# A ring place cleared behind every second transfer in a row, and two low parts moved from GpSimd to VectorE

## The chip, the cores and the metric

The kernel runs on one core of a Trainium2 chip, in one launch. The metric is the device time of that launch in microseconds (us), measured without a profiler. Besides, one execution was recorded by the hardware profiler; its clock starts at the first recorded instruction. The engines go by these names: PE is TensorE (PEld its weight loads), DVE is VectorE, ACT is ScalarE, POOL is GpSimd, SP is SyncE, which here only issues transfers.

## The reference

Pooled attention with 8 batches, 8 heads, 576 tokens, head width 64, followed by a routed feed-forward layer with 8 experts. All is float32.

```
k_p, v_p = mean over groups of 8 keys (576 -> 72)
attn     = softmax(q k_p^T / 8);  x = attn v_p        # 4608 tokens of 512 numbers
compute  = x @ w_skip > 0                              # the other tokens keep x
e        = argmax(x @ w_gate), g = its probability     # 8 experts
out      = x + g * (relu(x @ w1[e]) @ w2[e])           # 512 -> 1024 -> 512
```

## The kernel before, in words

**Numbers in two parts.** The expert products multiply float32 as a high and a low part: `whi` is the weight rounded by ACT (`high`, line 600), `wlo` the weight minus `whi` (`low` on POOL, line 603, or `low_v` on DVE, line 608). A chunk of weights (`cc` 0 to 7, 512 KB each; 0 to 3 are of w1, 4 to 7 of w2) comes from DRAM into a place of `stage`; each chunk is split in two halves `i` of 128 x 512.

**First stage: 36 tiles of attention.** The loop at line 866 takes one tile of 128 tokens a turn `t`, with scores, exponentials, transposes and values of different tiles overlapped. Tiles are routed in groups of 9, 5, 4, 6, 5, 4 and 3 (`route`, line 385): DVE finds each token's expert, PE counts ranks, DVE makes the places `r_di`, and POOL then writes one indirect transfer for each tile (line 433), which scatters 128 rows of 32 bytes (token number and gate weight) into `table` in DRAM. After the first group one expert is picked, the *early expert*. Three tiles of its tokens, from the first 18 tiles, are gathered by POOL at turn 30 (line 512) and computed while the routing ends; the writes of later tiles wait until those tokens are known.

**The order on POOL and DVE is planned when the program is built.** `Work` (line 642) holds items with the turn from which they can run, the turn at which they are due, and a cost; each turn it takes items up to a budget. `Spaced` (line 663) does this for POOL, and holds the table writes and the three gathers apart as `writes`. A write is taken if at least 1.2 us (`APART`) of other planned work was taken since the last one, or if no other item can run and the write is due. The writes of a group are due in successive turns. From turn 26 on, `fill` is set to `clear` (line 790): before a write that follows another one closely it puts a memset of one of the ring places 3 to 5 (128 x 516 numbers). These places must be zero before the experts stage, each at least once. After the last attention tile the rest is taken in two calls (lines 934 and 943), and the three writes of the last group in a third (line 982), where `fill` is off.

**Low parts.** `later_low` (line 702) is called when a half's high part is made. The first halves (`i` = 0) of chunks 2 to 6 and both of chunks 0 and 1 go to POOL; the second halves of chunks 2 to 6 go to DVE; chunk 7 is done after the routing on DVE (line 993). The first halves of chunks 5 and 6 have their turn on POOL at turns 33 and 35. When a place of `stage` has been split, SP loads into it a chunk of the second expert (`load_second`, line 590; chunk 7 goes to the place that chunk 5 had, at turn 35).

**From the routing to the experts.** PE has 56 steps of the early expert's two products (line 573) in hand. 36 of them are placed among the last routing work, the last 20 in the experts stage. Once the whole table is written, POOL gathers the rows that say which tokens each unit has (line 1070); PE transposes them (line 1102), DVE copies them to `slot` and `gate`, and after the steps that are left all engines meet at the entry of the experts stage (line 1137). There POOL gathers token rows by `slot` (line 1314), and from then on PE computes unit after unit. The order of PE in the program is fixed: line 1102 stands behind 28 of the 36 steps and ahead of the other 8.

Of the kernel before, what the change touches and what calls it, by code (L numbers as in the profile page):

```python
# [40 lines left out]
NT = NTOK // 128  # L41
# [19 lines left out]
WRITE, APART, REST = 1.27, 1.2, 0.5  # L61
# [27 lines left out]
def chunk_src(w1, w2, e, c):  # L89
    if c < 4:  # L90
        return w1[bass.ds(e, 1)].rearrange("o (p k) n -> k (o p) n", k=4)[c]
    k = (c - 4) * 2
    return w2[bass.ds(e, 1), k * 128:(k + 2) * 128, :].rearrange("o (a p) n -> (o p) a n", p=128)
# [6 lines left out]
def chunk_view(st, c):  # L100
    return st if c < 4 else st.rearrange("p (a n) -> p a n", a=2)
# [62 lines left out]
def attention(tc, nc, q, k, vm, vr, cf, wg, w1, w2, whi, wlo, out, c, pay, offs, table, near, bufs, late, early, mb, fin, cfs):  # L164
    with ExitStack() as ctx:
# [358 lines left out]
        later, now = {}, {}  # L524
# [54 lines left out]
        def expert(i, most=NE - 1):  # L579

            if i not in experts_:
                r = nc.sync.alloc_register(f"expert{i}")
                nc.sync.reg_load(r, near["order"][0:1, i:i + 1])
                experts_[i] = nc.sync.snap(r, min_val=0, max_val=most)
            return experts_[i]

        def room(cc):
            return 5 + cc % 3 if cc < 6 else (0, 5)[cc - 6]

        def load_second(c):  # L590
            nc.sync.dma_start(chunk_view(stage[:, c], c), chunk_src(w1, w2, expert(1), c))

        def load_first(cc):
            assert cc == 6 or len(lows) >= (8 if cc == 7 else 2 * cc - 4), (cc, lows)
            nc.sync.dma_start(chunk_view(stage[:, room(cc)], cc), chunk_src(w1, w2, expert(0), cc))

        def piece(w, cc, i):
            return w[0][:, cc, i * 512:i * 512 + 512] if cc < 4 else w[1][:, (cc - 4) * 2 + i, :]
# [4 lines left out]
        def low(cc, i):  # L603
            lows.append(cc)
            nc.gpsimd.tensor_tensor(piece(wlo, cc, i), stage[:, room(cc), i * 512:i * 512 + 512],
                                    piece(whi, cc, i).bitcast(F32), ALU.subtract)

        def low_v(cc, i):
            lows.append(cc)
            nc.vector.tensor_tensor(piece(wlo, cc, i), stage[:, room(cc), i * 512:i * 512 + 512],  # L610
                                    piece(whi, cc, i).bitcast(F32), ALU.subtract)
# [5 lines left out]
        class Queue:  # L617

            def __init__(self):
                self.gens, self.held = [], False  # L620
# [21 lines left out]
        class Work:  # L642
# [9 lines left out]
            def take(self, t, spent=0.0, most=99):  # L652
                got = [i for i in self.items if i[2] <= t]
                for i in got:
                    if most == 0 or spent + i[3] > self.budget and i[0] > t:
                        break
                    spent += i[3]
                    most -= 1
                    self.items.remove(i)
                    i[4]()  # L660
                return spent

        class Spaced(Work):

            def __init__(self, budget):
                super().__init__(budget)
                self.writes, self.apart, self.hold, self.fill = [], APART, True, None

            def write(self, ready, last, f, early=True):
                self.n += 1  # L670
# [3 lines left out]
            def take(self, t):  # L674
                spent = 0.0
                while True:
                    w = next((i for i in self.writes if i[2] <= t and (i[4] or not self.hold)), None)
                    o = next((i for i in self.items if i[2] <= t), None)
                    late = w is not None and w[0] <= t
                    if w is None and o is None or spent >= self.budget and not late and not (o is not None and o[0] <= t):  # L680
                        break
                    if w is not None and (self.apart >= APART or o is None and late):
                        if self.apart < REST and self.fill:
                            self.fill()
                        self.writes.remove(w)
                        w[3]()
                        spent, self.apart = spent + WRITE, 0.0
                    elif o is not None:
                        self.items.remove(o)
                        o[4]()  # L690
                        spent, self.apart = spent + o[3], self.apart + o[3]
                    else:
                        break

        loads, behind, turns = {}, {}, {}
        lows = []
        act, dve, gps = Work(ACT), Work(DVE), Spaced(GPS)
# [4 lines left out]
        def later_low(cc, i):  # L702
            if cc == 7:
                return
            if cc > 1 and i:
                dve.add(now["t"] + 1, now["t"] + 2, 0.65, lambda: low_v(cc, i))
                return
            gps.add(now["t"] + (2 if cc > 4 else 1), (NT if cc > 5 else wload(cc + 3)) - 1, 1.25, lambda: low(cc, i))

        def adds(b, ready, last):  # L710
            first, small = sums(b)
# [4 lines left out]
        def wload(cc):  # L716
            return PICKED + 9 * cc // 4 if cc < 8 else NT - 2
# [15 lines left out]
        for cc in range(8):  # L733
            (loads if cc else behind).setdefault(wload(cc), []).append(lambda cc=cc: load_first(cc))
            for i in range(2):
                act.add(wload(cc) + (3 if cc < 3 else 4), min(wload(cc) + 6, NT - 2), 0.55, lambda cc=cc, i=i: (high(cc, i), later_low(cc, i)))

        for cc, t in SECOND.items():
            at(t, lambda cc=cc: load_second(cc))
# [21 lines left out]
        o = ps_o.tile([128, 2, 512], F32, name="o")  # L761
# [104 lines left out]
        for t in range(2, NT):  # L866
# [35 lines left out]
            spent = act.take(t, 0.4 if new is not None else 0.0, 2 if t + 1 in FIRST[2:] else 1)  # L902
# [917 lines left out]
```

## Time and profile before

| | |
|---|---|
| median of 3 runs | 483.04 us (481.76 to 483.20) |
| the profiled execution | 483.0 us |
| its span, first to last instruction | 480.9 us |
| mean granted clock of TensorE | 0.993 |
| PE busy | 456.1 us (95%) |
| POOL busy | 251.0 us (52%) |
| DVE busy | 302.1 us (63%) |
| ACT busy | 226.8 us (47%) |

The profiled execution took 483.0 us; 2.1 us of it lie outside the span. Busy shares are means over all stages: POOL has 52% over the span, but in the stage before the experts it hardly rests.

### The profile page before, as it was taken

To read this page: it belongs to the slowest core of one execution; us is meant where nothing else is said; L and a number is where in the kernel's file an instruction comes from. 1 tells how busy PE (TensorE), PEld (TensorE's weight loads), DVE (VectorE), ACT (ScalarE), POOL (GpSimd) and SP (SyncE) were. 2 spreads that over 40 slices of the span, in tenths; PEclk is the share of its full clock that TensorE was granted. 3 is DMA by queue.
4 is the path that set the end of the run, shared out by engine and by line. 5 is a ranking of instruction groups with operands and counts; after the bars stand their busy time and mean duration, and the time that the engine had idled before them with its cause. 6 is when DMAs were issued, how large, how long until landed. Compare 5 with 4: busy or idle time off the path is not lost. (4 is left out here: it accounts for less than half of the span.)

```text
span 480.9 us, 12651 instructions
## 1 busy us (share of the span) xinstructions
PE 456.1 (95%) x3755; PEld 406.7 (85%) x3756; DVE 302.1 (63%) x713; ACT 226.8 (47%) x614; POOL 251.0 (52%) x328
## 2 busy tenths in 40 slices
PE   7899989999989589999999998999999999999995
PEld 4689888888989579888989987989899898989894
DVE  5878898789779113579795657662756654343321
ACT  5678889899951001447462746512435241212110
POOL 4499399999998145335242514352543161515242
PEclk9999999999999799999999999999999999999999
DMA  8999999979720016688677597877687323322021
GB/s 282 399 396 388 400 365 343 389 269 338 255 107 3 9 47 199 219 217 294 246 248 281 169 296 262 316 229 243 197 251 263 99 88 107 128 66 88 22 87 42
DMA packets 52048, 103.98 MB, mean 216 GB/s; under 512 B 10031, under 2 KB 22959, under 8 KB 50336
## 3 DMA queue, kind: packets, MB, share of 16 engines
q1 hardware_dynamic: 40544, 78.18, 47.1%
q0 software_dynamic: 11456, 25.22, 14.9%
q8 instruction: 23, 0.38, 0.3%
q14 instruction: 25, 0.20, 0.1%
HBM read 80.85 MB, written 31.21 MB: 233 GB/s over the span
## 5 line engine op out<-in xcount | busy, mean ns | idle before, releaser
L1319 POOL DMA_INDIRECT out<-ring,slot x33 | 35.4, 1073 | 106.0 <-POOLq L1145 102.9
L331 ACT ACTIVATE e<-sc,mn 128x72 f32<-128x72 f32 x288 | 65.5, 352 | 10.9 <-DVE mn L323 10.2
L1557 ACT ACTIVATE hhi<-psl 128x256 fp32r<-128x256 f32 (+3 forms) x59 | 23.5, 400 | 98.0 <-ACTq L1145 91.8
L1413 PE MATMUL psl<-xhi,w1hi 128*128 128x256 f32 (+3 forms) x220 | 64.0, 291 | 0.0
L1414 PE MATMUL psl<-xlo,w1hi 128*128 128x256 f32 (+3 forms) x220 | 64.0, 291 | 0.0
L1415 PE MATMUL psl<-xhi,w1lo 128*128 128x256 f32 (+3 forms) x220 | 63.9, 291 | 0.0
L1314 POOL DMA_INDIRECT ring<-out,slot x42 | 49.1, 1168 | 24.5 <-issue 24.1
L359 PE MATMUL o<-vbd,pT 128*128 128x148 f32 (+1 forms) x312 | 50.3, 299 | 4.9 <-ACT pT L346 1.8
L1656 DVE SCALAR_TENSOR_TENSOR hlo<-psl,hhi 128x256 fp32r<-128x256 f32 (+2 forms) x55 | 23.2, 423 | 42.9 <-DVEq L1145 39.7
L359 PEld LDWEIGHTS o<-vbd,pT 128*128 128x128 f32 (+1 forms) x312 | 39.2, 179 | 9.0 <-ACT pT L346 4.3
L1413 PEld LDWEIGHTS psl<-xhi,w1hi 128*128 128x128 f32 x220 | 41.3, 188 | 0.8 <-issue 0.4
L1414 PEld LDWEIGHTS psl<-xlo,w1hi 128*128 128x128 f32 x220 | 41.3, 188 | 0.5
L1415 PEld LDWEIGHTS psl<-xhi,w1lo 128*128 128x128 f32 x220 | 41.2, 187 | 0.0
L433 POOL DMA_INDIRECT table<-pay,r_di x36 | 36.3, 1009 | 6.4 <-issue 5.4
L1327 POOL DMA_DIRECT2D sorted<-ring x39 | 22.2, 571 | 32.7 <-DMA ring<-out,slot 27.9
L1633 DVE TENSOR_TENSOR w2lo<-stage,w2hi 128x1024 fp32r<-128x1024 f32 x28 | 34.2, 1222 | 6.8 <-DVEq L1145 5.3
L1414 PE MATMUL psd<-xlo,w1hi 128*128 128x256 f32 (+3 forms) x132 | 38.4, 291 | 0.0
L1415 PE MATMUL psd<-xhi,w1lo 128*128 128x256 f32 (+3 forms) x132 | 38.4, 291 | 0.0
L1413 PE MATMUL psd<-xhi,w1hi 128*128 128x256 f32 (+3 forms) x132 | 38.3, 290 | 0.0
L1439 PE MATMUL mb<-w2hi,hlo 128*128 128x512 f32 x88 | 34.8, 396 | 0.0
L1439 PE MATMUL psf<-w2hi,hlo 128*128 128x512 f32 x88 | 34.8, 396 | 0.0
L1437 PE MATMUL psf<-w2hi,hhi 128*128 128x512 f32 x88 | 34.8, 395 | 0.0
(278 smaller groups left out, 1202.5 us busy)
## 6 DMA issues: line engine op xcount, KB each, us to landing
stage<-in_w SPq DMA_DIRECT2D x64, 512.0 KB, 5.8
sorted<-ring POOLq DMA_DIRECT2D x39, 256.0 KB, 3.4
out<-x SPq DMA_DIRECT2D x36, 256.0 KB
stage<-in_k SPq DMA_DIRECT2D x6, 1152.0 KB
blocks<-sorted SPq DMA_DIRECT2D x100, 64.0 KB
qt<-in_q SPq DMA_DIRECT2D x9, 512.0 KB
hhi<-in_vm SPq DMA_DIRECT2D x4, 1024.0 KB
hlo<-in_vm SPq DMA_DIRECT2D x3, 1024.0 KB
```

Of the source, the lines that this page charges most:

```text
L331: nc.scalar.activation(ev[:, g % 2, k0:k0 + SP], sc[:, j * SP:(j + 1) * SP], AF.Exp, bias=mn[:, 4 * n + j:4 * n + j + 1], scale=-1.0)
L359: nc.tensor.matmul(o_[sl, g * 2 * VA:(g + 1) * 2 * VA], pT[a][:, g, sl], vbd[b % 2][:, 2 * a + g, :], start=(g == 0), stop=False)
L433: m = nc.gpsimd.indirect_dma_start(table, bass.IndirectOffsetOnAxis(ap=di[:, j:j + 1], axis=0), flat(fin["pays"][:, t0 + j:t0 + j + TW // ...
L1314: g.indirect_dma_start(ring[:, (s + 3) % 9, 0:D], None, out, bass.IndirectOffsetOnAxis(ap=slot[:, s:s + 1], axis=0), bounds_check=NTOK - 1 ...
L1319: g.indirect_dma_start(out, bass.IndirectOffsetOnAxis(ap=offsets, axis=0), ring[:, (s + 3) % 9, 0:D], None, bounds_check=NTOK - 1, oob_is_ ...
L1413: t.matmul(ps, whi[0][:, k, w], xhi[:, k, xs], start=(k == 0), stop=False)
L1414: t.matmul(ps, whi[0][:, k, w], xlo[:, k, xs], start=False, stop=False)
L1415: last = t.matmul(ps, wlo[0][:, k, w], xhi[:, k, xs], start=False, stop=(k == 3))
L1437: t.matmul(ps, hhi[:, k, sl], whi[1][:, k, :], start=(k == 0), stop=False)
L1439: last = t.matmul(ps, hlo[:, k, sl], whi[1][:, k, :], start=False, stop=(k == 7))
L1557: a.activation(hhi[:, f, xs], bank(f, xs, alone), AF.Relu).then_inc(sem["act"], 1)
L1633: v.tensor_tensor(chunk_of(wlo, c), chunk_view(stage[c], c), chunk_of(whi, c).bitcast(F32), ALU.subtract).then_inc(sem["wlo1" if c < 4 els ...
```

## The change

Two edits of the planner. `Spaced` counts the writes taken in a row (`row`), and puts a clear ahead of a write only when two writes have gone since the last clear or since other work; before, it put one ahead of every write that follows another within 0.5 us of planned work. And `later_low` gives the first halves of chunks 5 and 6 to DVE, ready one turn after their high part and due two turns after; before, POOL had them. The assertions of `load_second` and `load_first` are written anew to count the halves of the chunk whose place is used again.

```
 def load_second(c):
+    assert c < 5 or lows.count(c - 2) == 2
 def load_first(cc):
-    assert cc == 6 or len(lows) >= (8 if cc == 7 else 2 * cc - 4), (cc, lows)
+    assert cc in (0, 1, 2, 6) or lows.count(3 if cc == 7 else cc - 3) == 2
...
-    self.writes, self.apart, self.hold, self.fill = [], APART, True, None
+    self.writes, self.apart, self.hold, self.fill, self.row = [], APART, True, None, 0
...
 if w is not None and (self.apart >= APART or o is None and late):
-    if self.apart < REST and self.fill:
+    if self.row > 1 and self.fill:
         self.fill()
+        self.row = 0
     self.writes.remove(w)
     w[3]()
-    spent, self.apart = spent + WRITE, 0.0
+    spent, self.apart, self.row = spent + WRITE, 0.0, self.row + 1
 elif o is not None:
     self.items.remove(o)
     o[4]()
-    spent, self.apart = spent + o[3], self.apart + o[3]
+    spent, self.apart, self.row = spent + o[3], self.apart + o[3], 0
...
 def later_low(cc, i):
     if cc == 7:
         return
-    if cc > 1 and i:
+    if cc > 1 and i or cc > 4:
         dve.add(now["t"] + 1, now["t"] + 2, 0.65, lambda: low_v(cc, i))
         return
-    gps.add(now["t"] + (2 if cc > 4 else 1), (NT if cc > 5 else wload(cc + 3)) - 1, 1.25, lambda: low(cc, i))
+    gps.add(now["t"] + 1, wload(cc + 3) - 1, 1.25, lambda: low(cc, i))
```

## Rows read from the trace of the kernel before

**Rows 1.** Busy time by stretch: PE, PEld, DVE, ACT, POOL, PEclk, DMA share, GB/s.

```profile
140.00:157.50 17.50, 16.12 (x97) 15.25 (x95) 15.02 (x72) 3.03 (x7) 14.57 (x18) 1.00 0.10 32
163.10:171.40 8.30, 7.11 (x26) 6.22 (x26) 1.95 (x6) 0.49 (x1) 0.00 (x0) 0.75 0.00 0
```

**Rows 2.** Timeline of PE: start us, length us, line, [idle before <-releaser].

```profile
125.54 0.72 PE L359 MATMUL o<-vbd,pT 128*64 128x148 f32 x8 [0.18 <-DVE x L378]
...
155.24 0.44 PE L550 MATMUL sc<-xhi,w1hi 128*128 128x384 f32 x1 [0.83 <-DVE hlo L558]
...
157.25 0.34 PE L552 MATMUL sc<-xhi,w1lo 128*128 128x384 f32 x1
163.07 0.51 PE L1102 MATMUL o<-cfs,stage 81*128 81x81 f32 x2 [5.48 <-issue]
163.31 0.67 PE L550 MATMUL sc<-xhi,w1hi 128*128 128x384 f32 x1
...
167.25 0.40 PE L568 MATMUL mb<-w2hi,hhi 128*128 128x512 f32 x1
...
171.44 0.50 PE L568 MATMUL mb<-w2hi,hhi 128*128 128x512 f32 x1 [1.23 <-issue]
```

**Rows 3.** Timeline of POOL, from the early gathers to the gather of rows.

```profile
120.34 1.14 POOL L512 DMA_INDIRECT ring<-out,nslot  x1 [0.28 <-POOL nslot L517]
...
127.70 1.00 POOL L433 DMA_INDIRECT table<-pay,r_di  x1 [0.17 <-issue]
128.72 1.29 POOL L605 TENSOR_TENSOR w2lo<-stage,w2hi 128x512 fp32r<-128x512 f32 x1
130.18 0.99 POOL L433 DMA_INDIRECT table<-pay,r_di  x1 [0.17 <-issue]
...
136.05 1.16 POOL L433 DMA_INDIRECT table<-pay,r_di  x1 [0.17 <-issue]
...
149.73 0.98 POOL L433 DMA_INDIRECT table<-pay,r_di  x1 [0.17 <-issue]
...
151.41 0.99 POOL L433 DMA_INDIRECT table<-pay,r_di  x1 [0.17 <-issue]
...
155.28 1.36 POOL L433 DMA_INDIRECT table<-pay,r_di  x1 [0.30 <-issue]
158.72 1.08 POOL L1070 DMA_INDIRECT stage<-table,s_coli  x1 [2.08 <-DMA table<-pay,r_di]
```

**Rows 4.** POOL by line from 120 to 157: count, busy us, mean ns, idle before.

```profile
L433 POOL DMA_INDIRECT table<-pay,r_di x18 | 18.3, 1017 | 3.4 <-issue 2.8 <-DVE s_last L1090 0.3 <-DVE lg L380 0.2
L792 POOL MEMSET ring<- 128x516 f32 x15 | 8.3, 551 | 0.0
...
L605 POOL TENSOR_TENSOR w2lo<-stage,w2hi 128x512 fp32r<-128x512 f32 x2 | 2.6, 1286 | 0.0
```

**Rows 5.** Timeline of DVE, from turn 30 to the end of the routing.

```profile
115.69 0.97 DVE L610 TENSOR_TENSOR w2lo<-stage,w2hi 128x512 fp32r<-128x512 f32 x1
...
123.75 0.21 DVE L373 RECIPROCAL rc<-o 128x8 f32<-128x8 f32 x1 [0.17 <-PE o L362]
...
131.07 0.21 DVE L373 RECIPROCAL rc<-o 128x8 f32<-128x8 f32 x1 [0.45 <-PE o L362]
...
135.66 0.68 DVE L610 TENSOR_TENSOR w2lo<-stage,w2hi 128x512 fp32r<-128x512 f32 x1
...
144.49 0.17 DVE L426 RECIPROCAL pay<-r_se 128x3 f32<-128x3 f32 x1
...
146.58 0.75 DVE L1043 TENSOR_SCALAR s_none<-s_units 128x8 f32<-128x8 f32 x1
...
150.13 0.16 DVE L1069 TENSOR_TENSOR s_coli<-s_col 128x1 int32<-128x1 f32 x1
...
155.10 1.28 DVE L610 TENSOR_TENSOR w2lo<-stage,w2hi 128x512 fp32r<-128x512 f32 x2
```

**Rows 6.** Timeline of SP: the load of the second expert's chunk 7.

```profile
130.04 0.40 SPq L591 DMA_DIRECT2D stage<-in_w  x1
```

More of the change, by code (lines that the diff above doesn't have):

```diff
@@ L590, in load_second @@
         def load_second(c):
+            assert c < 5 or lows.count(c - 2) == 2
             nc.sync.dma_start(chunk_view(stage[:, c], c), chunk_src(w1, w2, expert(1), c))
         def load_first(cc):
-            assert cc == 6 or len(lows) >= (8 if cc == 7 else 2 * cc - 4), (cc, lows)
+            assert cc in (0, 1, 2, 6) or lows.count(3 if cc == 7 else cc - 3) == 2
             nc.sync.dma_start(chunk_view(stage[:, room(cc)], cc), chunk_src(w1, w2, expert(0), cc))
@@ L666, in __init__ @@
                 super().__init__(budget)
-                self.writes, self.apart, self.hold, self.fill = [], APART, True, None
+                self.writes, self.apart, self.hold, self.fill, self.row = [], APART, True, None, 0
             def write(self, ready, last, f, early=True):
@@ L682, in take @@
                     if w is not None and (self.apart >= APART or o is None and late):
-                        if self.apart < REST and self.fill:
+                        if self.row > 1 and self.fill:
                             self.fill()
+                            self.row = 0
                         self.writes.remove(w)
                         w[3]()
-                        spent, self.apart = spent + WRITE, 0.0
+                        spent, self.apart, self.row = spent + WRITE, 0.0, self.row + 1
                     elif o is not None:
@@ L690, in take @@
                         o[4]()
-                        spent, self.apart = spent + o[3], self.apart + o[3]
+                        spent, self.apart, self.row = spent + o[3], self.apart + o[3], 0
                     else:
@@ L704, in later_low @@
                 return
-            if cc > 1 and i:
+            if cc > 1 and i or cc > 4:
                 dve.add(now["t"] + 1, now["t"] + 2, 0.65, lambda: low_v(cc, i))
                 return
-            gps.add(now["t"] + (2 if cc > 4 else 1), (NT if cc > 5 else wload(cc + 3)) - 1, 1.25, lambda: low(cc, i))
+            gps.add(now["t"] + 1, wload(cc + 3) - 1, 1.25, lambda: low(cc, i))
         def adds(b, ready, last):
```

## The prediction

> **What bounds the kernel now.** I read the page first: PE is busy nearly all the time, so time is to be had only where PE waits or where its clock is down. Then I went through the span by stretches. Up to 157.5 us the granted clock is 1.00, the upper of its two levels (2.4 GHz); in the stretch that follows the early expert's first product it is 0.75, a mean over both levels (1.2 and 2.4 GHz) [rows 1]. PE's timeline shows why: after the matmul that starts at 157.25 PE does nothing until 163.07, a gap of 5.48 us, the longest of the kernel, ahead of the transposes of line 1102 [rows 2]. The profile names "issue" there, so the releaser is something it doesn't show, and line 1102 needs the rows that POOL's transfer of line 1070 brings.
>
> Followed back on POOL: that transfer starts at 158.72, after 2.08 us of waiting for the last table write to land; the last write was issued at 155.28 and took 1.36 us [rows 3]. Its places were ready long before: DVE finished the last group's values at 144.49 + 0.17 = 144.66, and the indices of line 1070 at 150.13 + 0.16 = 150.29 [rows 5]. So the writes wait for their turn on POOL, not for data. From 120 to 157 POOL issues 3 gathers and 18 writes, with 15 clears of 551 ns and two low parts of 1286 ns between them; its idle ahead of the 18 writes is 3.4 us in all [rows 4]. The path that sets the end is therefore: POOL's row of issues from 120.34, landing, line 1070, landing, PE at 163.07. After PE's meeting with the other engines (it resumes at 171.44 after 1.23 us [rows 2]) I found no wait of comparable size, so I take what follows as shifting with it.
>
> **The clears.** I put the new rule on the order that the trace shows, since late writes are taken only when due, and nothing is moved forward by a free budget. The three gathers stand in a row: one clear, ahead of the third. The first write makes it two in a row, then the short memset of line 801 ends the row. Second to fifth write: one clear, ahead of the fourth. Then the writes go on in a row without other work: five of the second group mixed with the last of the first, four of the third group, with a clear ahead of every second one, five more in all. The last three have none, as before. That makes 1 + 1 + 5 = 7 clears where there are 15, 8 fewer; each of the three places is still cleared.
>
> What one costs: an issue with a clear ahead of the next is followed by the next after 151.41 - 149.73 = 1.68 us; the four that have no clear between them stand (155.28 - 151.41) / 3 = 1.29 us apart [rows 3]. So a clear costs 0.39 us, not its 0.55, since part of it lies in a pause that two issues have between them anyway. 8 x 0.39 = 3.12 us. Bound below: nothing, if a longer row of issues without clears makes each as slow as with one; above: 8 x 0.55 = 4.4 us. I take 3.12, as it is measured on the same instruction and the new rule has pairs, mostly, where the trace has four.
>
> **The two low parts off POOL.** With a low part between them two writes start 130.18 - 127.70 = 2.48 us apart instead of 1.29 [rows 3]: 1.19 each, 2.38 for both. Both places get a due write next, so the writes close up.
>
> **The two low parts on DVE.** One takes 0.68 us there (135.66), 0.97 where it met POOL's arithmetic (115.69) [rows 5]. Chunk 5's falls behind the minima of turn 32; next on DVE is the reciprocal at 123.75, which had waited 0.17 us for PE. Chunk 6's falls behind turn 34, ahead of the reciprocal at 131.07, which had waited 0.45 us [rows 5]. What is late next is DVE's product `x`, for which PE waits 0.18 us at 125.54 [rows 2], and the minima for ACT. I charge PE 0.2 us in all; bounds nothing, and 2 x 0.97 = 1.94 if all cover is gone. The routing steps of these turns are not put off: at turn 32 one step is taken either way, and at turn 34 none is there.
>
> SP: the load of chunk 7 is issued at 130.04 [rows 6], just when POOL's low part of chunk 5 ends (128.72 + 1.29 = 130.01 [rows 3]). It can now go sooner, with the outputs behind it. The second expert needs it after 171 us, so I count nothing; that cover is more than 40 us.
>
> **POOL and DVE at once.** The write at 136.05 took 1.16 us beside a low part at 135.66, against 0.98 at 149.73; the last one took 1.36 us beside two low parts of chunk 7 at 155.10 [rows 3, 5]. The other way round a small DVE operation took 0.75 us at 146.58 [rows 5]. So each moved low part may stretch an issue by 0.18 to 0.38 us; I take 0.18, so 0.36 for two. And the last issue will be over before the low parts of chunk 7 come: 1.36 - 0.98 = 0.38 us back. These cancel.
>
> The Trainium skill (SBUF — State Buffer, "SBUF: two separate sides") says that DVE and GpSimd share one pair of ports as an exclusive lock, held for a whole instruction, by DVE operations in a two-port mode or with two SBUF inputs, the latter only against a GpSimd operation that reads SBUF. That speaks against giving DVE work while POOL is the bound: by the full lock each moved low part would hold up POOL for its length, and 1.36 us would come off the sum instead of 0.36. The stretched rows agree that the two hinder each other, but with less than the full length.
>
> **The sum.** The issues end 3.12 + 2.38 = 5.50 us sooner, at 155.28 - 5.50 = 149.78 for the last; the indices (150.29) are ready before the table has landed, so line 1070 follows at 158.72 - 5.50 = 153.22 and PE could start line 1102 at 163.07 - 5.50 = 157.57. PE comes there at 157.25 + (157.25 - 155.24) / 11 = 157.43 [rows 2], plus the 0.2 of the tile loop: 157.63. So both arrive together and the gap closes: 163.07 - 157.63 = 5.44 us.
>
> Then the clock. The 12 matmuls behind line 1102 take 167.25 - 163.31 = 3.94 us at the lowered clock; the 12 from 155.24, just as wide and at 1.00, take 2.01 x 12 / 11 = 2.19 us. What PE did before its clock fell was to idle; it idled 0.83 us at 155.24 in the stretch with 1.00 [rows 1, 2]. Without the long gap I expect no fall: 1.75 us back. Together 5.44 + 1.75 = 7.19 us. The profiled execution, 483.0 us (the median of the runs is 483.04, so the same number serves), becomes 475.8 us.
>
> Its own range: at best the wait of 0.83 us goes too, as DVE's operations meet fewer issues, and the rows come 0.4 us sooner (the last issue at its short length with no stretching): 163.07 - 157.17 + 1.75 = 7.65, and some more where a clear is worth its 0.55; I end at 474.6. At worst a low part is not covered and a gap of 1 us stays: 477.3.
>
> **The rivals.**
> - *The clears were free* (0.12). If issues without clears are spaced as with them, only the low parts count: 2.38 - 0.36 = 2.0 us, 481.0; with part of the clock back up to 3.8 us, 479.2. For it speaks that the fourth in a row was the longest; against it the even 1.29 us of three intervals.
> - *The port lock* (0.10). The stretching of the rows, but by the whole length of a low part: 2 x (0.68 - 0.18) = 1.0 us more of gap, 476.8 us, and 477.1 if DVE's low parts get longer as well. The rule of the Trainium skill named above gives this time.
> - *The gap closes, but the clock falls all the same, or fewer clears go* than I count (0.08): 483.0 - 5.44 = 477.6; four clears fewer instead of eight leave 1.56 us, 477.4.
> - *Another wait takes its place* (0.06). Line 1102 also needs PE's bank and the meeting of all engines at 171.44 may hang on something I don't see, as its 1.23 us is put down to "issue" alone. Then the whole gain is lost there: 483.0, no change. Against: ACT and DVE have nothing left there but what follows PE's own matmuls.
> - *Issues in a row block POOL* (0.06), the case on the other side. If POOL may have only so many descriptors under way, an issue that follows another at once waits for the earlier to drain, and the clears gave that time. It is slower by over 1.45 us when the 8 intervals without clear cost (2.38 + 1.45) / 8 = 0.48 us more than 1.68, so 2.16 us or more: 484.5 and up. For it speaks only the 1.36 us at 155.28, and that has the low parts of chunk 7 beside it; against it the 1.29 us.
>
> **The numbers.** My forecast has 0.58. What this kernel's measurement can tell from no change is about 0.3%, 1.45 us. Faster by more: 0.58 + 0.12 + 0.10 + 0.08 = 0.88; within: 0.06; slower: 0.06. The range from 474.4 to 479.6 holds the forecast, the lock, the clock case and the nearer part of the free clears, some 0.8.
>
> **What would show it.** POOL with 7 clears and no low part from 120 to 157; writes 1.29 us apart in pairs and 1.68 between pairs; the last write near 149.8 and line 1070 near 153.2; line 1102 near 157.6 with a wait under 1 us; clock 1.00 behind it, and 2.2 us for its 12 matmuls; DVE's low parts near 123.2 and 130.6 with PE late by under 0.3 us at the end of the tiles. The prediction is wrong if issues without clears are spaced by 1.6 us or more, if line 1102 waits though line 1070 came early, or if the meeting at the stage's entry doesn't move with PE.

## The result, and the profile after

The change took 476.61 us (median of 4 runs, 474.27 to 477.01), the kernel before 483.12 us (4 runs, 481.76 to 483.64): a ratio of 0.986, with a 95% interval of 0.9822 to 0.9898. That is 6.5 us less; 7.2 were forecast. In the sets of runs behind it the change measured 0.9856 (0.9825 to 0.9887) and 0.9847 (0.9794 to 0.99) on two chips, and 1.0082 (1.0049 to 1.0115) on a third, of which the experiments tell. The ratios of that chip leave out the runs that lie more than 1.5% above the kernel's fastest, and so say less than the medians do.

One thing has to be taken off before the rows are compared: in the profiled execution of the change the first gather starts at 121.85, against 120.34 [rows 3]. This execution was late by 1.51 us before anything that was changed. Times "less 1.51" are set against the forecast.

POOL's timeline after (start us, length us, line, [idle before <-releaser]), which answers to [rows 3]:

```profile
121.85 1.14 POOL L512 DMA_INDIRECT ring<-out,nslot  x1 [0.28 <-POOL nslot L517]
123.28 1.02 POOL L512 DMA_INDIRECT ring<-out,nslot  x1 [0.30 <-issue]
124.29 0.55 POOL L794 MEMSET ring<- 128x516 f32 x1
125.01 1.23 POOL L512 DMA_INDIRECT ring<-out,nslot  x1 [0.17 <-issue]
...
128.09 1.20 POOL L433 DMA_INDIRECT table<-pay,r_di  x1 [0.16 <-issue]
...
135.56 0.99 POOL L433 DMA_INDIRECT table<-pay,r_di  x1 [0.30 <-issue]
136.53 0.56 POOL L794 MEMSET ring<- 128x516 f32 x1
137.26 1.43 POOL L433 DMA_INDIRECT table<-pay,r_di  x1 [0.17 <-issue]
138.99 0.98 POOL L433 DMA_INDIRECT table<-pay,r_di  x1 [0.30 <-issue]
...
150.49 0.98 POOL L433 DMA_INDIRECT table<-pay,r_di  x1 [0.30 <-issue]
151.78 0.98 POOL L433 DMA_INDIRECT table<-pay,r_di  x1 [0.30 <-issue]
154.84 1.08 POOL L1072 DMA_INDIRECT stage<-table,s_coli  x1 [2.08 <-DVE hlo L558]
```

Grouped by line from 121.85 to 152.8 (count, busy us, mean ns, idle before), as [rows 4] of before:

```profile
L433 POOL DMA_INDIRECT table<-pay,r_di x18 | 18.4, 1022 | 4.5 <-issue 3.7 <-DVE l L377 0.3 <-DVE s_more L1050 0.3
L794 POOL MEMSET ring<- 128x516 f32 x7 | 3.9, 554 | 0.0
```

Seven clears instead of fifteen, and no low part among the groups: eight clears and both low parts have left POOL's row, as put on record. From the first gather to the last write it is 151.78 - 121.85 = 29.93 us, against 155.28 - 120.34 = 34.94. Issues stand 1.29 us apart in a pair (150.49 to 151.78); with a clear between them they stand 1.70 apart (135.56 to 137.26). The last issue took 0.98 us instead of 1.36. The "DVE hlo" that the last row names is only what happened to end then; in the kernel before the same wait of 2.08 us is put down to the landing of the table write.

PE's timeline after, as [rows 2], and the busy time of the stretch behind the transposes (PE, PEld, DVE, ACT, POOL, PEclk, DMA share, GB/s), as the second line of [rows 1]:

```profile
127.05 0.72 PE L359 MATMUL o<-vbd,pT 128*64 128x148 f32 x8 [0.19 <-DVE x L378]
...
157.64 0.34 PE L552 MATMUL sc<-xhi,w1lo 128*128 128x384 f32 x1
159.27 0.42 PE L1104 MATMUL o<-cfs,stage 81*128 81x81 f32 x2 [1.29 <-issue]
...
161.66 0.40 PE L568 MATMUL mb<-w2hi,hhi 128*128 128x512 f32 x1
...
165.87 0.50 PE L568 MATMUL mb<-w2hi,hhi 128*128 128x512 f32 x1 [1.26 <-issue]
```

```profile
159.27:165.87 6.60, 5.34 (x26) 4.45 (x26) 1.95 (x6) 0.49 (x1) 0.00 (x0) 1.00 0.00 0
```

The wait ahead of the transposes (line 1104 now) fell from 5.48 to 1.29 us, the granted clock behind it is 1.00 instead of 0.75, and from the transposes to the first matmul of line 568 it is 2.39 us instead of 4.18. PE leaves the meeting of the engines at 165.87, less 1.51: 164.36, against 171.44, so 7.08 us earlier.

DVE's timeline after, as [rows 5]:

```profile
124.68 0.68 DVE L611 TENSOR_TENSOR w2lo<-stage,w2hi 128x512 fp32r<-128x512 f32 x1
...
127.73 0.68 DVE L611 TENSOR_TENSOR w2lo<-stage,w2hi 128x512 fp32r<-128x512 f32 x1
...
132.04 0.68 DVE L611 TENSOR_TENSOR w2lo<-stage,w2hi 128x512 fp32r<-128x512 f32 x1
...
137.15 0.68 DVE L611 TENSOR_TENSOR w2lo<-stage,w2hi 128x512 fp32r<-128x512 f32 x1
...
148.06 0.17 DVE L1045 TENSOR_SCALAR s_none<-s_units 128x8 f32<-128x8 f32 x1
```

The two low parts that DVE took over are those at 124.68 and 132.04, at 0.68 us each, and PE's wait for `x` behind the first is 0.19 us, as before (0.18).

### The profile page after: what moved, and what is told of

Read it like the earlier page. It is cut to its first block, busy times and chain, and to the rows that moved or that the text cites. A ratio compares the mean times of both kernels' runs of the same rounds, so it can differ in the third digit from the quotient of the medians.

```text
span 475.1 us, 12640 instructions
## 1 busy us (share of the span) xinstructions
PE 453.7 (95%) x3755; PEld 405.1 (85%) x3756; DVE 302.4 (64%) x715; ACT 227.0 (48%) x614; POOL 244.6 (51%) x318
```

## The experiments

Theory: the path to the transposes goes through POOL's row of issues; each clear between two issues costs about 0.4 us, each low part about 1.2, and the long wait also costs 1.75 us of clock. Rivals: the low parts alone do it; the clock's share is given back later; fewer clears hurt. All runs were made in three sets, each on one chip, with the kernel before run in between: its medians were 483.61, 482.56 and 482.99 us. Each set was made once, so that a chip and the time of its set can't be told apart.

### The set on which the change was slower

The change once more:

> The changed kernel once more, to size its gain on the same chip as the other runs. By the trace of its first run the gain is 7.1 us where PE resumes at the entry of the experts stage, if the 1.51 us by which that execution was already late at turn 30 (ahead of anything that was changed) is not part of it. Theory: the late start is scatter of the first loads of keys, so a new profile has it or not, and the stretch from the first early gather to the last table write is 29.9 us again (34.9 before). Rival: the change itself makes the start late, then every profile of a changed kernel shows it, and none of the kernel before.

The rule for the clears alone, with the low parts left on POOL:

```
-    if self.apart < REST and self.fill:
+    if self.row > 1 and self.fill:
         self.fill()
+        self.row = 0
```

> The new rule for clears alone; POOL keeps the two low parts, which also break a row, so there are 6 clears instead of 15. Theory (a clear costs 0.39 us on POOL's path): 9 x 0.39 = 3.5 us less from the first early gather to the last write, 31.4 us; PE's wait ahead of the transposes of the row list about 2.0 to 2.8 us instead of 5.5; time 3.5 us below before if the clock still falls, 5.2 us if it doesn't. Rival (the clears were free, the low parts paid it all): the stretch stays near 34.9 us and the time at that of before.

The low parts alone, with the old rule for the clears:

```
-    if cc > 1 and i:
+    if cc > 1 and i or cc > 4:
```

> The two low parts alone go to DVE; the old rule for clears stands, which then also puts clears where the low parts were, 17 instead of 15. Theory: two intervals of 2.48 us become 1.68 each, 1.6 us less, minus some 0.4 to 0.6 us for issues that DVE's low parts stretch, so the stretch from first gather to last write is 33.7 to 33.9 us, PE's wait some 4.3 us and the time 1.0 to 1.6 us below before, with the clock still down. Rival (the low parts paid it all): stretch near 30 us and the time 6 us below before.

The change with all three places cleared at once in turn 10, and no clear among the issues:

```
+    gps.add(10, 10, 1.4, lambda: nc.gpsimd.memset(bufs["ring"][:, TILES:2 * TILES], 0.0))
...
-    if t == FILLS:
-        gps.fill = clear
```

> The changed kernel, but the three ring places are cleared by one memset at turn 10, where POOL has room, and no clear stands between the issues: 21 issues in a row but for one short memset. Theory (0.39 us for each of the 7 clears left): stretch 29.9 - 2.7 = 27.2 us, the row list is there before PE comes, so PE's wait of 1.29 us goes and no more: some 1.3 us below the changed kernel. Rival (issues in a row block POOL): the stretch does not get shorter, single issues or pauses of over 1.6 us appear, and the time is that of the changed kernel or above.

Measured against the kernel before on the same chip: the change 491.88 us, 1.0082 (1.0049 to 1.0115); clears alone 486.02, 1.0014 (0.9974 to 1.0054); low parts alone 482.0, 0.9968 (0.9938 to 0.9997); all cleared early 489.28, 1.0103 (1.0064 to 1.0142). None of the three kernels with fewer clears is faster here, and two are slower: the opposite of the theory. The profiles show where. In the profiled execution of the change (495.43 us) the first gather is on time (120.65), but the last write is issued at 168.32, 47.67 us later instead of 29.93. With the clears alone this stretch is 38.08 us, with the low parts alone 35.40 and with all cleared early 40.91, where 31.4, 33.7 to 33.9 and 27.2 were expected. POOL is not the cause, for it waits for DVE; the tile loop itself stalls. The longest of these waits of POOL in the change, and its busy time by stretch there:

```profile
142.64 0.98 POOL L433 DMA_INDIRECT table<-pay,r_di  x1 [10.16 <-DVE l L377]
```


```profile
110.00:120.00 10.00, 8.88 (x151) 7.90 (x149) 8.03 (x18) 7.83 (x27) 9.68 (x15) 0.95 0.49 162
120.00:130.00 10.00, 7.80 (x71) 7.04 (x71) 4.49 (x17) 3.33 (x12) 8.31 (x11) 0.83 0.79 275
130.00:140.00 10.00, 7.54 (x88) 7.11 (x89) 5.54 (x20) 6.06 (x24) 2.17 (x3) 0.66 0.35 122
```

PE, DVE and ACT all have idle time, and the clock falls to 0.66. One cause can be read; POOL, DVE and PE at 117 us:

```profile
117.37 1.27 POOL L606 TENSOR_TENSOR w2lo<-stage,w2hi 128x512 fp32r<-128x512 f32 x1
118.61 1.03 POOL L271 TENSOR_TENSOR vbd<-vs,cfs 128x512 f32<-128x512 f32 x1
119.64 0.73 POOL L517 TENSOR_SCALAR nslot<-nids,less 128x3 int32<-128x3 f32 x1
```

```profile
117.32 2.87 DVE L611 TENSOR_TENSOR w1lo<-stage,w1hi 128x512 fp32r<-128x512 f32 x1
...
130.46 0.82 DVE L323 TENSOR_REDUCE mn<-sc 128x4 f32<-128x288 f32 x2 [4.40 <-PE pt L262]
```

```profile
121.46 1.33 PE L359 MATMUL o<-vbd,pT 128*128 128x148 f32 x4 [2.59 <-DVE x L378]
```

A low part that takes 0.68 us alone took 2.87, as long as POOL had one operation behind the other; PE then waited 2.59 us for DVE, and its next matmuls ran at the lower clock. Another low part had taken 3.00 us at 102.75, and with the low parts alone one took 3.02 at 102.83: all ahead of the first write or gather of which the order was changed. What stands behind the 4.40 us at 130.46 the profile doesn't show. DVE's minima there need scores that PE had issued at 125.30, and the releaser named comes later. With all cleared early the same wait is 5.12 us, with no long low part ahead of it. So there are at least two kinds of stall. The kernel before took its usual time on this chip, 483.61 us, but was not profiled here, so that it is free of them is argued from its time alone. That the changed order alone makes them is excluded by the second and third sets below; what this chip adds stays open.

### The change beside the kernel before, and the price of the wait

> The kernel before, unchanged, for its profile on the chip of the runs beside it. If the stalls of the tile loop that the last profiles show (TensorE's signals two to six microseconds late between 95 and 150 us) come from the chip and not from the changed order, they stand here too, one or two of them, and the time is 481 to 487 us; if fewer clears cause them, this profile has none and the first gather to the last table write takes 34.9 us, as in the first profile.

> The change, unchanged. Theory: the order on GpSimd saves five microseconds from the first gather to the last table write, and the time is 474 to 478 us against 483, unless the tile loop stalls. Rival: fewer clears make the tile loop stall, and the time is 485 to 492 us on any chip.

The kernel before, with matmuls in the gap whose results nobody reads (put in one place here; in the kernel they stand in a function of their own):

```
     tp = psum()
+    for _ in range(28):
+        nc.tensor.matmul(os_hot[:, 0:384], whi[0][:, 0, 0:128], bufs["xhi"][:, 0], start=True, stop=True)
     for i in range(2):
         nc.tensor.transpose(tp[:, i, 0:SLOTS], ...)
```

> The kernel before, with 28 matmuls more on TensorE, whose results nobody reads, in the gap ahead of the transposes at line 1102. If the clock at 0.50 is a price of that gap by itself, it stays at 1.00, the 12 matmuls after the transposes take 2.2 us instead of 3.9 and the time is 481.3 us against 483.1. If the 1.75 us are given back later, or the fillers delay the transposes, it is 483.1 us or more.

The change, with POOL held up ahead of the row gather:

```
     nc.vector.tensor_tensor(coli, col[:, 1:2], col[:, 2:3], ALU.add)
+    for _ in range(8):
+        nc.gpsimd.memset(bufs["ring"][:, 3], 0.0)
     nc.gpsimd.indirect_dma_start(rows, None, table..., coli...)
```

> The change, with eight clears of one ring place more on GpSimd between the last table write and the row gather: 2.4 us of delay by the clears' own length, and nothing else. If the row gather sets when TensorE goes on, its wait grows from 1.29 to about 3.7 us and the time from 476.6 to 479.0 us, with the clock at 1.00; if a wait of that length drops the clock as in the kernel before, 480.8 us. If something else ends that wait, 476.6 us.

The change took 475.24 us (0.9856, 0.9825 to 0.9887), and neither profile has the stalls of the first set. Chance put the first gathers of the two profiles at almost the same time, so they can be read side by side. POOL and PE of the kernel before:

```profile
120.81 1.14 POOL L512 DMA_INDIRECT ring<-out,nslot  x1 [0.28 <-POOL nslot L517]
...
155.78 1.36 POOL L433 DMA_INDIRECT table<-pay,r_di  x1 [0.30 <-issue]
159.23 1.07 POOL L1070 DMA_INDIRECT stage<-table,s_coli  x1 [2.09 <-DMA table<-pay,r_di]
```

```profile
155.74 0.44 PE L550 MATMUL sc<-xhi,w1hi 128*128 128x384 f32 x1 [0.85 <-DVE hlo L558]
163.26 0.51 PE L1102 MATMUL o<-cfs,stage 81*128 81x81 f32 x2 [5.16 <-issue]
171.64 0.50 PE L568 MATMUL mb<-w2hi,hhi 128*128 128x512 f32 x1 [1.26 <-issue]
```

And of the change:

```profile
120.83 1.14 POOL L512 DMA_INDIRECT ring<-out,nslot  x1 [0.28 <-POOL nslot L517]
...
150.78 0.98 POOL L433 DMA_INDIRECT table<-pay,r_di  x1 [0.30 <-issue]
153.86 1.07 POOL L1072 DMA_INDIRECT stage<-table,s_coli  x1 [2.09 <-DVE hlo L558]
```

```profile
157.82 0.42 PE L1104 MATMUL o<-cfs,stage 81*128 81x81 f32 x2 [0.84 <-issue]
164.39 0.50 PE L568 MATMUL mb<-w2hi,hhi 128*128 128x512 f32 x1 [1.23 <-issue]
```

The last write comes 5.00 us sooner, the row gather 5.37, the transposes 5.44, the resumption 7.25. The 1.81 us between the last two are the clock: 1.00 behind the transposes of the change, 0.76 behind those of the kernel before.

The kernel with PE kept busy took 480.9 us, 0.9979 (0.9954 to 1.0005): 1.7 us less by the medians, of the size expected, but the interval reaches to no change. Its profile has the clock at 1.00 behind the transposes and 2.31 us from them to the first of line 568's matmuls. That execution is the slowest of its ten, at 484.6 us, and its tile loop ran late (first gather at 123.92). The fillers ended at 167.47, 5.45 us after the start of the row gather, where 3.96 to 4.43 us do in the change: there they cost over 1 us of what they gave. The other nine were not profiled. So that the clock costs the whole run its 1.75 us is read from the traces and not shown by this experiment.

The delayed gather is clear: 479.48 us, 0.9936 (0.9914 to 0.9958), 4.24 above the change. Its POOL, its PE, and its busy time from 158 to 170:

```profile
152.11 0.98 POOL L434 DMA_INDIRECT table<-pay,r_di  x1 [0.30 <-issue]
153.08 4.66 POOL L1074 MEMSET ring<- 128x516 f32 x8
158.21 1.08 POOL L1075 DMA_INDIRECT stage<-table,s_coli  x1 [0.47 <-issue]
```

```profile
162.29 0.51 PE L1107 MATMUL o<-cfs,stage 81*128 81x81 f32 x2 [3.98 <-issue]
...
166.52 0.63 PE L569 MATMUL mb<-w2hi,hhi 128*128 128x512 f32 x1
```

```profile
158.00:170.00 12.00, 7.93 (x28) 6.66 (x26) 1.95 (x6) 0.98 (x2) 1.08 (x1) 0.72 0.04 9
```

From the last write to the row gather it is 6.10 us instead of 3.08: 3.02 us of delay, where 2.4 were put on record. PE's wait grew from 0.84 to 3.98, and the clock fell: 4.23 us from the transposes to line 568 instead of 2.39. So the row gather sets when PE goes on, and in this execution, the slowest of ten (482.38 us), the wait has its price in clock on top. Not every execution paid it. By the last row the fall takes 12.00 x (1 - 0.72) / 480 = 0.007 off the mean clock (an estimate), but three of the ten executions have a mean of 0.998 or 0.999; they took 478.19 to 479.16 us, 3.0 to 3.9 above the change, which is near the delay alone. Of the two prices on record the median's 4.24 us equals the one with the clock (480.8 - 476.6 = 4.2 us), but in part by chance, since 3.02 of it is delay.

### The parts on another chip, where the change is faster

The same two parts and the early clear, with the change beside them:

> The new rule for the clears alone, the two low parts left on GpSimd: 6 clears instead of 17. Theory: 11 clears less at 0.39 us take 4.3 us from the stretch between the first gather and the last table write (34.97 us in the kernel before), the clock stays at 1.00, and the time is 476.5 us where the kernel before takes 482.6. Rival, from the runs on the other chip: fewer clears make the tile loop stall, 485 us.

> The old rule for the clears, the two low parts on VectorE. Theory: two low parts at 1.19 us leave GpSimd and two clears at 0.39 us come in, so that the stretch is 1.6 us shorter; TensorE still waits over 3 us, so the clock still falls, and the time is 481 us. Rival: VectorE's two low parts cost the tile loop what they free on GpSimd, 482.6 us.

> The change with one clear of the three ring places in turn 10 and none among the issues. Theory: the last table write comes 2.7 us earlier than in the change, TensorE's remaining wait of 0.84 us goes and nothing more, because TensorE's own work then sets the end: 474.4 us, 0.8 below the change. Rival, from the run on the other chip: issues without clears stall the tile loop, 487 to 489 us.

> The change, beside its two parts on one chip. Where the tile loop runs without stalls, 474 to 477 us, and the parts' gains (6.0 and 1.6 us by the theory) add up to about its gain of 7.3. Where it stalls as on the one other chip, 486 to 495 us, and the first gather is followed by gaps of GpSimd of two microseconds and more that end with VectorE.

| kernel | median us | ratio (95%) | first gather to last write | wait ahead of the transposes |
|---|---|---|---|---|
| before, on the chip of the second set | 482.56 | 1 | 34.97 | 5.16 |
| clears alone | 477.56 | 0.9899 (0.9859 to 0.9939) | 31.34 | none |
| low parts alone | 479.9 | 0.9952 (0.9927 to 0.9978) | 33.28 | 2.05 |
| the change | 474.36 | 0.9847 (0.9794 to 0.99) | 29.96 | 1.01 |
| all cleared early | 474.32 | 0.9835 (0.9788 to 0.9883) | 27.17 | none |

The ratios are against the kernel before on the same chip (482.99 us); the first row is of another. The expectation for the clears alone had a wrong count: with the low parts on POOL the kernel before has 15 clears, not 17, so 9 go. 9 x 0.39 = 3.5 us fits the 3.63 measured. The gains in per cent add up within their intervals: 1.01 + 0.48 = 1.49, the change 1.53.

The waits of the clears alone and of the low parts alone can't be set beside the others. A transpose of the tile loop (line 341) that starts at 137.34 in the change came late in these two executions, as did the first gather (121.75 and 122.89, against 120.84), but by less:

```profile
140.92 0.33 PE L341 MATMUL pt<-cfs,e 128*128 128x128 f32 x1 [0.39 <-ACT e L331]
142.05 0.33 PE L341 MATMUL pt<-cfs,e 128*128 128x128 f32 x1 [0.38 <-ACT e L331]
```

PE is late by 3.6 and 4.7 us, POOL by 0.9 and 2.1. So PE lost some 2.7 us against the row of issues, and without that the waits would be about 2.6 and 4.7 us (an estimate from these rows), where 2.0 to 2.8 and over 3 were put on record. The low parts alone gain 3.1 us by the medians, the 1.69 of their stretch and more; how much of the rest is clock is not shown. Long low parts of DVE are not the first chip's alone either. The kernel with the low parts alone has this one here:

```profile
119.64 2.79 DVE L611 TENSOR_TENSOR w2lo<-stage,w2hi 128x512 fp32r<-128x512 f32 x1
```

The kernel with the clears alone has one of 1.56 us. What did not come here are the waits of the second kind.

With 7 clears fewer than the change, the early clear saves 29.96 - 27.17 = 2.79 us, 0.40 each. Issues in a row without any clear don't block POOL; from 120 us on (last write, row gather, and PE at the transposes):

```profile
147.69 0.98 POOL L433 DMA_INDIRECT table<-pay,r_di  x1 [0.30 <-issue]
150.75 1.07 POOL L1070 DMA_INDIRECT stage<-table,s_coli  x1 [2.08 <-DVE s_odd L1082]
```

```profile
156.51 0.34 PE L1102 MATMUL o<-cfs,stage 81*128 81x81 f32 x2
...
196.87 0.49 PE L1424 MATMUL psf<-w2hi,hhi 128*128 128x512 f32 x1 [1.26 <-PEq L1145]
```

PE comes to the transposes without a wait, so the row of issues is no longer what it waits for, as expected. The time is that of the change all the same. PE resumed 1.57 us before the change did (163.03 against 164.60), and 0.76 of it goes at 196.87, where it waits 1.26 us and the change 0.50. Where the other 0.8 goes is not shown.

This also settles a part of what was open in the first set: the kernels of the change and of the early clear, which took 491.88 and 489.28 us there, take 474.4 and 474.3 here. The order is not slow by itself; why it was slow there is not shown.

## Why the prediction was right, step by step

- *The clears*: 8 fewer, as put on the order. 0.39 us each was forecast; 0.40 came out of 9 and of 7 clears. The rival "the clears were free" is excluded by the clears alone (0.9899), "issues in a row block POOL" by the early clear.
- *The two low parts off POOL*: 1.19 each. Alone, two clears came in, so (1.69 + 2 x 0.40) / 2 = 1.24 each.
- *Low parts on DVE*: 0.2 us was charged to PE; its wait for `x` rose by 0.01. Their cover held in the executions where the tile loop ran freely.
- *POOL and DVE at once*: the term that was mis-sized, and its mechanism was read wrongly. The prediction took the 1.16 and 1.36 us of [rows 3] for a hindrance of less than a low part's length. The rows show a full hold for what is left of the low part: the write at 136.05 ends at 137.21, 0.87 us behind the end of the low part that was running (135.66 + 0.68 [rows 5]). After the change the issues at 125.01, 128.09 and 137.26 end 0.88, 0.88 and 0.86 us behind the ends of the low parts at 124.68, 127.73 and 137.15. In all these profiles 29 issues begin inside a low part of 0.68 us that stands by itself, and each ends 0.85 to 0.89 us behind its end; an issue that begins ahead of the low part keeps its 0.98 (131.28, beside the low part at 132.04). So one low part costs POOL between nothing and about 0.5 us, by where an issue meets it. Here three issues took longer than their like: the third gather 1.23 us (the three gathers of before took 1.06 on the mean), and two writes, 1.20 against 1.00 and 1.43 against 1.16 [rows 3], beside low parts that DVE had before too; in the kernel before no issue began inside the first of these, and the one inside the second began later in it. That is about 0.2 + 0.2 + 0.27 = 0.67 us more, where the forecast had 0.36 and let it cancel against the 0.38 of the last issue. That the two are no further apart is luck. The last write was issued 5.01 us sooner instead of 5.50; the 0.38 came back as forecast (0.98 instead of 1.36), and the row gather came 5.39 us sooner (5.50 forecast).
- *The rival of the full lock* had the mechanism and not the price. By the rule of the Trainium skill (SBUF — State Buffer, "SBUF: two separate sides") whichever of the two engines' operations starts first has the shared ports for its whole instruction, and the other blocks. The trace agrees for the issues, with the 0.85 to 0.89 us above; the whole 0.68 us for each moved low part did not come, since an issue meets only what is left of one. On the side of DVE the low part of 2.87 us at 117.32 agrees in kind; but it ends 0.55 us behind the second of two operations of POOL (117.37 and 118.61), so it was kept waiting by more than one instruction.
- *The sum*: row gather 153.22 forecast, 154.84 - 1.51 = 153.33 measured; transposes 157.63, measured 157.76; clock 1.75, and 4.18 - 2.39 = 1.79; together 7.19, and 7.08 or, side by side, 7.25. By the medians the three sets gave 6.5, 7.3 and 8.6 us, so the nearness of the first to the forecast says less than these rows do.
- *A wait that I kept went too*: PE's 0.83 us for `hlo` [rows 2] is not among its waits now. In the kernel before small DVE operations of the routing took 0.75 us (146.58 [rows 5]); the same one takes 0.17 now, at 148.06. DVE's chain is shorter, PE arrives 1.3 us sooner than forecast, and therefore shows a wait of 1.29 where I had none. It changes nothing at the end, as the rows set it. The operation of 0.75 us ends with the write that POOL issued meanwhile (146.35 + 0.98 = 147.33); but the one at 148.06 begins inside an issue too (147.92 to 148.90) and is not stretched. What decides between the two is not shown.
- *The range* held on three sets of four. None of the rivals named the stalls of the tile loop, and the change's price on that one chip is outside the range.

## What to carry to other kernels

When an engine's row of transfer issues is what the next stage waits for, price its fillers by the interval from issue to issue, with and without them, not by their own length: 0.55 us of clear cost 0.40. Where VectorE has operations like these low parts (two inputs in SBUF), their cost to GpSimd is set by the order of starts: an issue that began first was not stretched, one that began second was held until they ended. A long wait of TensorE can be dearer than it looks, when the matmuls behind it run at the lower clock: in the two profiles side by side 5.4 us of gap cost 7.2. And run such a change on more than one chip: this one gave 1.4 to 1.5% on three sets of runs, and took 0.8% on a fourth.

## What the runs showed that was not expected

- The granted clock behind a wait of PE: 1.00 after waits of 0.84, 1.01 and 1.29 us, and 12 matmuls with their transposes took 2.39 us; after 2.05 us (low parts alone) they took 3.80, after 3.98 and 5.48 us 4.2.
- A DVE subtraction with two inputs in SBUF, 0.68 us alone, took 0.96 to 3.02 us where POOL ran arithmetic without a pause, on all three chips, and 0.68 beside POOL's transfer issues, which it held up until it ended (0.98 us alone, 1.50 at most, with the low parts alone).
- On one chip waits of 4.4 and 5.1 us in the tile loop for which the trace shows no late work. They remain unexplained.
